# Reordering the front of an attention and top-1 MoE kernel: casts, clears, slot list, unread products and a nested general path

## The chip, the cores and the metric

The kernel runs on one core of a Trainium2 chip. The metric is the device time of one execution in microseconds. It is quoted as the median of several runs. The profile comes from one of these runs. Its times count from the start of its span, which is some 1.7 us shorter than the device time. Every run also lists the clock that TensorE was granted.

## The reference

Attention with two separate softmaxes feeds a top-1 mixture of experts.

```python
# q, k, v: (8 batches, 8 heads, 576, 64), fp32
q_s = softmax(q, over the 64 features);  k_s = softmax(k, over the 576 positions)
kv = einsum('bhsd,bhse->bhde', k_s, v)
x = einsum('bhsd,bhde->bhse', q_s, kv)  -> reshaped to (4608 tokens, 512)

logits = x @ w_gate + modality_bias[modality_id]      # 8 experts, 2 modalities
e_idx = argmax(logits);  gate_w = softmax(logits)[e_idx]
out[token] = gate_w * (relu(x @ w1[e_idx]) @ w2[e_idx])   # 512 -> 1024 -> 512
```

With this draw the modality bias decides the expert, so two experts serve all tokens. The kernel's fast path holds just these two. A general path over all experts stands at the end of the program and is entered only if a check on the chip fails. It runs zero times here.

## The kernel before

For each of the eight batches the program does the following. `prep` computes `exp(k)` and `exp(q)` on ACT and casts v to bf16. `attend` forms the kv product on TensorE (PE), scales it on DVE (`kvbd`), turns q (`tp_ps` to `et`) and kv (`kvT_ps` to `kvT`), and from these the gate products `g_ps` and the logits `lg_ps`. `route` picks the expert, counts the tokens (`r_ps`), scales the tokens (`x_sb`), sorts them by a permutation product (`xT_ps`), and ACT copies them into windows of the sorted buffer `xs`, one expert from the left and one from the right. `slots` and `places` make the list that says where each row of the output goes (`hv`, `hlo`, `id_ps`). The FFN is 148 pieces of PE work on `xs`, called by `mains(n)` or spread by `weave` among the steps of a batch. PE is programmed in a fixed order, so a piece that waits holds all behind it.

The parts that the change touches (`...` marks a cut):

```python
    xs = persist.tile([P, KD, NSLOT], BF16)          # 128 x 4 x 4864: the sorted tokens
    ...
    def clear(b):                                     # zero places of batch b, both sides
        lo, hi = S * b, min(S * (b + 1), NSLOT // 2)
        xs_w[b] = [
            nc.gpsimd.memset(xs[:, :, c : c + hi - lo].bitcast(FP32), 0.0) for c in (lo, NSLOT - hi)
        ]
    clear(0)
    clear(1)
    ...
    def cast_weights(s, part, eng):                   # fp32 stage buffer -> bf16 W, 128 x 2048
        copy_on(eng, W[:, s, part * 2 * F : (part + 1) * 2 * F], wst.pop((s, part))[:, 0 : 2 * F])
    ...
    steps(a1, 4)
    token_ids()
    cast_weights(0, 0, nc.gpsimd)
    for _ in range(NT - 1):
        steps(r0, 1)                                  # batch 0 sorted
        steps(a1, 1)                                  # batch 1 attended
    alone(r0)
    cast_weights(0, 1, nc.scalar)
    alone(a1)
    mains(1)                                          # the first FFN piece
    r1 = route(1)
    cast_weights(0, 2, nc.scalar)
    ...
    steps(r1, 1)
    slots(0)                                          # slot list of batch 0
    cast_weights(1, 0, nc.gpsimd)
    for b in range(2, 5):
        clear(b)                                      # six memsets in a row
    mains(1)
    places(0)                                         # the product that reads slots(0)
    mains(1)
    weave([next(r1)], 0.6)
    cast_weights(1, 1, nc.vector)
    weave(r1, 0.6)
    cast_weights(1, 2, nc.scalar)
    cast_weights(1, 3, nc.scalar)
    mains(12 - now[0])
    slots(1)
    ...
    with tc.For_i(0, nr) as e:                        # general path: nr is 0 here
        ...
        for _, _, lo, w in passes:                    # unrolled: 19 column groups
            hT = hbuf.tile([P, KF, GW], BF16, name="hT")
            alone(ffn1(xs[:, :, lo : lo + w], w, weights_of(0)[0], hT))
            alone(ffn2(w, weights_of(0)[1], hT, lambda: rows_of(sel1, lo, w), "stores again"))
```

The softmax here doesn't subtract the row's maximum and nothing guards it: scores larger than these inputs give would overflow.

## Time and profile before

| | before |
|---|---|
| device time, median of 3 runs | 267.23 us (265.94 to 267.35) |
| span of the profiled run | 265.6 us |
| PE busy | 200.6 us, 76% |
| DVE, ACT, GpSimd busy | 57%, 58%, 30% |
| PE busy between 45 and 60 us | 6.7 of 15 us |

PE is the bound for most of the span, so the time to win is where PE waits or runs at half clock. The row of busy tenths by slice shows that this is the first quarter. The marks to follow are the kv products: each batch begins with 36 of them, so their start times tell how far the program has come.

### The profile page before, as it was taken

The page shows a single profiled execution, that of the slowest core. Times are in us where ns is not written, and L with a number is a line of the kernel's source. Part 1 is how long each engine was busy: PE and PEld are TensorE (multiplying, and loading weights), DVE is VectorE, ACT ScalarE, POOL GpSimd, SP SyncE. Part 2 cuts the span into 40 slices and gives each one's busy share as a digit, 9 for nine tenths or more (in the row PEclk, how much of TensorE's full clock was granted, in tenths as well). Part 3 has the DMA queues.
Part 4 walks back from the last instruction along what each step waited for, and adds up shares of the span by engine and source line. Part 5 has one row for each costly group of instructions (what it writes and reads, how often), then busy time and mean ns, then how long its engine had stood idle before and what let it go on. Part 6 is the DMA issues. An engine that isn't in the chain of part 4 may idle for free. (4 is left out here: it accounts for less than half of the span.)

```text
span 265.6 us, 5231 instructions
## 1 busy us (share of the span) xinstructions
PE 200.6 (76%) x1934; PEld 137.4 (52%) x1954; DVE 151.4 (57%) x501; ACT 153.8 (58%) x241; POOL 78.7 (30%) x94
## 2 busy tenths in 40 slices
PE   0465668447898978898797899888788979999900
PEld 0354545135666447545565575566456637676500
DVE  7488573783043848876793967579385855311110
ACT  2977378138798559666666777665744634443300
POOL 8301000765114216022602341180142052141410
PEclk9995557759799999999999999999999999999975
DMA  6999999566999942861774010210102003030210
GB/s 233 371 390 404 393 391 321 200 206 234 356 389 343 355 174 50 346 237 64 238 246 172 2 79 0 81 79 2 42 12 111 0 39 121 0 158 2 110 57 1
DMA packets 18940, 46.58 MB, mean 175 GB/s; under 512 B 1229, under 2 KB 1229, under 8 KB 18910
## 3 DMA queue, kind: packets, MB, share of 16 engines
q1 hardware_dynamic: 15920, 36.70, 38.9%
q0 software_dynamic: 2960, 9.44, 8.8%
q8 instruction: 17, 0.28, 0.4%
q14 instruction: 13, 0.11, 0.1%
q10 hardware_dynamic: 30, 0.05, 0.1%
HBM read 36.75 MB, written 9.70 MB: 175 GB/s over the span
## 5 line engine op out<-in xcount | busy, mean ns | idle before, releaser
L726 PE MATMUL h_ps<-xs,W 128*128 128x256 bf16 x576 | 74.2, 282 | 4.7 <-ACT hT L737 2.7
L744 PE MATMUL y_ps<-W,hT 128*128 128x512 bf16 x268 | 68.9, 386 | 1.3 <-issue 0.3
L757 POOL DMA_INDIRECT out_dram<-y_sb,ix x37 | 36.7, 991 | 111.9 <-DVE y_sb L358 29.9
L726 PEld LDWEIGHTS <-W 128*128 128x128 bf16 x576 | 55.7, 101 | 14.3 <-issue 3.6
L737 ACT ACTIVATE hT<-h_ps 128x512 bf16<-128x512 f32 x73 | 42.0, 596 | 21.1 <-PE h_ps L726 20.3
L629 ACT CAST xs<-xT_ps 128x512 f32 (+2 forms) x80 | 38.8, 563 | 13.6 <-PE xT_ps L617 13.3
L744 PEld LDWEIGHTS <-hT 128*128 128x128 bf16 x296 | 26.9, 98 | 25.2 <-issue 1.1
L358 ACT COPY y_sb<-y_ps 128x512 f32<-128x512 f32 x22 | 12.9, 586 | 43.2 <-PE y_ps L744 40.9
L580 DVE TENSOR_TENSOR x_sb<-x_ps,qi 128x512 bf16<-128x512 f32 (+1 forms) x40 | 29.8, 764 | 1.2 <-PE x_ps L509 0.5
L358 DVE COPY y_sb<-y_ps 128x512 f32<-128x512 f32 x15 | 10.4, 692 | 33.0 <-PE y_ps L744 33.0
L659 POOL TENSOR_TENSOR hv<-hhi,vals 128x570 bf16<-128x570 bf16 x8 | 12.5, 1568 | 46.3 <-DVE hhi L655 42.5
L617 PE MATMUL xT_ps<-perm,x_sb 128*128 128x128 bf16 (+1 forms) x160 | 16.6, 232 | 9.2 <-DVE x_sb L580 6.6
L617 PEld LDWEIGHTS <-x_sb 128*128 128x128 bf16 (+1 forms) x160 | 10.9, 106 | 19.3 <-DVE x_sb L580 15.2
L376 ACT ACTIVATE ek<-st 128x1152 bf16<-128x1152 f32 x16 | 18.6, 1172 | 1.6 <-DMA st<-in_k_dram 1.6
L376 ACT ACTIVATE eq<-st 128x1152 bf16<-128x1152 f32 x16 | 18.4, 1158 | 0.6 <-DMA st<-in_q_dram 0.6
L509 PE MATMUL x_ps<-kvbd,et 128*128 128x128 bf16 (+1 forms) x160 | 17.5, 239 | 0.4 <-DVE et L358 0.4
L393 PE MATMUL kv_ps<-vb,ek 64*128 64x129 bf16 x288 | 12.8, 239 | 5.9 <-DVE vb L358 2.8
L429 PE MATMUL tp_ps<-ident,eq 128*128 128x128 bf16 x144 | 13.6, 241 | 4.1 <-DVE x_sb L580 2.4
L429 PEld LDWEIGHTS <-eq 128*128 128x128 bf16 x144 | 11.3, 109 | 9.1 <-issue 5.9
L393 PEld LDWEIGHTS <-ek 64*128 64x128 bf16 x288 | 10.3, 104 | 9.7 <-issue 7.6
L358 POOL CAST vb<-st 128x1152 bf16<-128x1152 f32 x12 | 13.5, 1152 | 0.0
L509 PEld LDWEIGHTS <-et 128*128 128x128 bf16 (+1 forms) x160 | 11.8, 109 | 3.3 <-issue 2.2
(148 smaller groups left out, 217.4 us busy)
## 6 DMA issues: line engine op xcount, KB each, us to landing
st<-in_k_dram SPq DMA_DIRECT2D x8, 1152.0 KB, 5.9
st<-in_moe_w_dram SPq DMA_DIRECT2D x8, 1024.0 KB, 12.6
st<-in_v_dram SPq DMA_DIRECT2D x7, 1152.0 KB, 6.3
st<-in_q_dram SPq DMA_DIRECT2D x6, 1152.0 KB, 5.7
st<-in_q_dram SPq DMA_DIRECT2D x4, 576.0 KB, 12.9
st<-in_v_dram SPq DMA_DIRECT2D x2, 576.0 KB, 8.1
out_dram<-y_sb,ix POOLq DMA_INDIRECT x37, 2.8
W<-in_moe_modality_id_dram ACTq DMA_DIRECT2D x1, 36.0 KB
```

Of the source, the lines that this page charges most:

```text
L358: return (nc.scalar.copy if eng is nc.scalar else eng.tensor_copy)(out=out, in_=in_)
L376: nc.scalar.activation(out=view((eks if nm == "k" else eqs)[b], [[Dh, 2], [HG * Dh, NJ], [1, Dh]], 2 * g * Dh), in_=src[:, 2 * g : 2 * g + ...
L393: nc.tensor.matmul(out=kv[hg][:, 130 * hp : 130 * hp + 129], lhsT=ek[rows, j, P * hp : P * hp + P], rhs=vb[rows, j, hp, 0:129], start=(j = ...
L429: nc.tensor.transpose(out=view(tp[c0], [[2 * nj * 64, 2], [1, 64]], hp * nj * 64 + jj * 64), in_=eq[:, c0 + jj, P * hp : P * hp + P], iden ...
L509: nc.tensor.matmul(out=view(x_ps, [[2 * Dh, 2], [1, Dh]], (4 * (p_ % 2) + p_ // 2) * Dh, (0, T)), lhsT=et[:, p_, tcol[t] : tcol[t] + T], r ...
L580: nc.vector.tensor_tensor(out=view(x_out[t], [[2 * Dh, HG], [Dh, 2], [1, Dh]], 0, (0, T)), in0=view(xps[t], [[2 * Dh, HG], [Dh, 2], [1, Dh ...
L617: nc.tensor.matmul(out=xT_ps[:, kd, 0:T], lhsT=x_out[t][0:T, kd * P : (kd + 1) * P], rhs=perm[0:T, t, 0:T], start=True, stop=True,)
L629: w = nc.scalar.copy(out=window(a + off, b, T, off > 0), in_=xT_ps[:, :, 0:T])
L726: nc.tensor.matmul(out=h_ps[:, f * w : (f + 1) * w], lhsT=w1(kd * F + (f0 + f) * P, P), rhs=x_in[:, kd, :], start=(kd == 0), stop=(kd == K ...
L737: nc.scalar.activation(out=h_out, in_=h_in, func=ACT.Relu)
L744: nc.tensor.matmul(out=y_ps, lhsT=hT[:, kf, t * P : (t + 1) * P], rhs=w2(kf * D, D), start=(kf == 0), stop=(kf == KF - 1),)
L757: store = nc.gpsimd.indirect_dma_start(out=out, out_offset=bass.IndirectOffsetOnAxis(ap=ix[:, t : t + 1], axis=0), in_=y_sb, in_offset=Non ...
```

## The change

The intent is to fill the holes of the first 75 us: weight casts go from ACT to idle GpSimd, the clears leave the middle of the program, the slot list of batch 0 is made earlier, and products whose result nobody reads keep PE busy in its waits. The general path is made small by a nested loop. The FFN pieces are also spread a little differently.

```diff
-    clear(0)
-    clear(1)
+    xs_w = [nc.gpsimd.memset(xs[:, kd, :].bitcast(FP32), 0.0) for kd in (2, 3)]
+    xs_w.append(nc.scalar.copy(out=xs[:, 0, :].bitcast(FP32), in_=view(modf, [[0, NSLOT // 2]])))
+    xs_w.append(nc.vector.memset(xs[:, 1, :].bitcast(FP32), 0.0))
 ...
-        tps, tag = (ff, "ff") if b == 0 else (mm, "mm")
+        tps, tag = (ff, "ff") if b < 2 else (mm, "mm")
-        yield 3
+        yield 2.6
-        yield 5
         scale(1)
+        yield 4.2
-            yield 1.2 if t < NT - 1 else 1.3
+            yield 1.4 if t < NT - 1 else 2
 ...
+    def busy(n):
+        junk = ff.tile([P, 512], FP32, name="junk", tag="ff")
+        for _ in range(n):
+            nc.tensor.matmul(out=junk[:, 0:P], lhsT=ones, rhs=tri, start=True, stop=True)
 ...
     r0 = route(0)
+    busy(12)
     steps(r0, 1)
+    busy(10)
 ...
     steps(a1, 4)
+    cast_weights(0, 0, nc.gpsimd)
+    cast_weights(0, 1, nc.gpsimd)
 ...                                   (steps of r0 and a1 with busy(4) to busy(6) between)
     token_ids()
+    slots(0)
     steps(a1, 1)
+    busy(6)
     alone(a1)
+    busy(12)
+    cast_weights(0, 2, nc.scalar)
     mains(1)
     r1 = route(1)
     steps(r1, 1)
-    mains(1)
+    mains(2)
     cast_weights(0, 3, nc.scalar)
     steps(r1, 1)
-    mains(2)
-    steps(r1, 1)
-    slots(0)
-    cast_weights(1, 0, nc.gpsimd)
-    for b in range(2, 5):
-        clear(b)
-    mains(1)
     places(0)
     mains(1)
-    weave([next(r1)], 0.6)
-    cast_weights(1, 1, nc.vector)
-    weave(r1, 0.6)
-    cast_weights(1, 2, nc.scalar)
-    cast_weights(1, 3, nc.scalar)
-    mains(12 - now[0])
+    cast_weights(1, 0, nc.gpsimd)
+    cast_weights(1, 1, nc.gpsimd)
+    steps(r1, 1)
+    mains(2)
+    cast_weights(1, 2, nc.gpsimd)
+    cast_weights(1, 3, nc.gpsimd)
+    weave(r1, 0.8)
     slots(1)
+    mains(14 - now[0])
 ...
-            if i == 6 and b > 2:
+            if i == 7 and b > 2:
                 places(b - 1)
-        weave(batch(b), (14 if b == 2 else 15.5) / 28.6, ...)
+        weave(batch(b), (12 if b == 2 else 15.5) / 28.9, ...)
 ...                                   (general path)
-        for _, _, lo, w in passes:
+        with tc.For_i(0, NSL, GW // P) as at:
+            x_in = hbuf.tile([P, KF, GW], BF16, name="hT")[:, 0:KD, :]
+            nc.vector.tensor_copy(out=x_in, in_=xs[:, :, ds(at * P, GW)])
+            sel2 = small.tile([P, GW // P], FP32, name="sel2")
+            nc.vector.tensor_copy(out=sel2, in_=sel1[:, ds(at, GW // P)])
             hT = hbuf.tile([P, KF, GW], BF16, name="hT")
-            alone(ffn1(xs[:, :, lo : lo + w], w, weights_of(0)[0], hT))
-            alone(ffn2(w, weights_of(0)[1], hT, lambda: rows_of(sel1, lo, w), "stores again"))
+            alone(ffn1(x_in, GW, weights_of(0)[0], hT))
+            alone(ffn2(GW, weights_of(0)[1], hT, lambda: rows_of(sel2, 0, GW), "stores again"))
```

## The prediction

> **What bounds the kernel now.** I first read the busy tenths by slice on the page.
>
> ```profile
> PE   0465668447898978898797899888788979999900
> ...
> PEclk9995557759799999999999999999999999999975
> ```
>
> A slice is 6.64 us. From slice 11 on TensorE (PE) is 80 to 90% busy at full clock; before that it is half idle and mostly at half clock. The table of stretches sizes both regimes.
>
> ```profile
> 45.00:52.00 7.00, 2.85 (x16) 0.99 (x14) 5.03 (x17) 0.58 (x2) 3.90 (x3) 0.89 0.70 271
> 52.00:60.00 8.00, 3.88 (x27) 2.47 (x25) 7.04 (x6) 3.13 (x7) 5.27 (x7) 0.50 0.65 184
> ...
> 125.00:150.00 25.00, 20.65 (x219) 13.93 (x220) 18.21 (x55) 17.02 (x29) 7.34 (x7) 1.00 0.51 174
> ...
> 225.00:250.00 25.00, 24.84 (x184) 16.77 (x186) 5.61 (x13) 10.42 (x18) 5.84 (x6) 1.00 0.15 61
> ```
>
> Columns: length, busy us of PE, PE weight load, DVE, ACT, POOL, then PE clock, DMA share, GB/s. The end (225 to 253) is dense FFN. The middle (six batches, 75 to 222) has PE 83 to 88% busy. In 45 to 60 PE works 6.7 of 15 us. The chain of waits is no help: it stops at the last store. So I went through the timeline of the front.
>
> ```profile
> 22.61 2.22 PE L393 MATMUL kv_ps<-vb,ek 64*128 64x129 bf16 x36 [0.42 <-ACT vb L358]
> ...
> 38.12 1.46 PE L726 MATMUL h_ps<-xs,W 128*128 128x256 bf16 x6 [1.70 <-ACT W L358]
> ...
> 49.80 0.52 PE L676 MATMUL id_ps<-hv,hlo 64*128 64x114 bf16 x5 [4.10 <-POOL hv L659]
> ...
> 51.52 4.56 POOL L228 MEMSET xs<- 128x1152 f32 x6
> ...
> 52.01 4.09 DVE L690 TENSOR_SCALAR ix<-sel 128x2 int32<-128x2 f32 x1
> ...
> 56.19 0.61 PE L617 MATMUL xT_ps<-perm,x_sb 128*128 128x128 bf16 x4 [3.52 <-DVE x_sb L580]
> ...
> 67.29 6.19 PE L726 MATMUL h_ps<-xs,W 128*128 128x256 bf16 x40 [2.69 <-ACT hT L737]
> ...
> 75.61 1.20 PE L393 MATMUL kv_ps<-vb,ek 64*128 64x129 bf16 x36
> ```
>
> Columns: start, duration, engine, what, and in brackets the idle time before it with its releaser. Four holes: the first FFN piece waits for a weight cast that stands late in ACT's queue; the slot list waits for `hv`, whose DVE chain (46.7 to 48.8) came too late; six clears of `xs` on GpSimd hold a 2-element DVE instruction for 4.09 us and all behind it; two weight casts on ACT (63.03 to 66.74) hold the ReLU. The first and last lines are the same 36 products, cold and warm: 2.22 against 1.20 us.
>
> **What the Trainium skill says.** (1) "SBUF — State Buffer", section "Who interferes with whom": DVE shares one port pair with GpSimd under an exclusive lock; a 2-port DVE copy or tensor_scalar fully blocks behind any GpSimd operation, one with two SBUF inputs only behind a GpSimd operation that reads. The trace agrees: under the memsets the two-input `ab` took its normal 0.19 us, the tensor_scalar `ix` 4.09; under the W cast at 49.69 the two-input `idb` took 0.90 instead of 0.20. (2) "TensorE: Matmul & The Clock Gate", Part 1: the clock is half until about one 3.4 us window is busy, and falls back after an idle one. The trace agrees: recorded clock 0.50 from 20 to 43 us and again in 52 to 60. (3) "VectorE: DVE Perf Modes", section "Zero memsets can be issued as uint32": a memset takes a cycle per element. Here 256 words took 0.27 us. (4) "Runtime: NRT & Kernel Launch", section "Instruction fetch mechanics": a taken branch beyond the prefetched pages stalls for a fetch. Here GpSimd's branch over the general path, at 257.8, is followed by nothing until 260.5, while the other engines went on.
>
> **The change part by part.**
>
> *Clearing.* All of `xs` is now cleared at the start, one quarter each on DVE and ACT and two on GpSimd. DVE: 2432 words at 0.27/256 = 2.55 us, from 8.0 (after `krow`) to 10.6, so the first `vb` cast moves from 9.10 to 10.6. ACT: copies take 0.59 for 512 and 1.90 for 2048 columns, so about 2.25 us for 2432; it starts at 4.8 where ACT waited 1.6 us for k, so it delays `ek` by 0.7 us. GpSimd: 2 x 2432 against 4 x 1152 words, 4.4 us for 4.14. Net cost on the path: kv products about 1.2 us late, and so everything to the first `lg_ps` (18.9 instead of 17.7), the bias product being moved into a wait. Cost: **+1.2**. What it removes: the memsets at 51.5, i.e. the 3.5 us hole.
>
> *Weight casts.* Seven of eight casts stood on ACT (five), DVE (one, blocked 4.48) and GpSimd (two); now six are on GpSimd at 1.89 each and two on ACT. W part 1 is cast as it lands, near 28 to 30 (estimate: part 0 was there at 25.3, and 1.05 MB at the 398 GB/s of that stretch take 2.6 us), so the 1.70 us wait goes. The last two slot-1 casts leave ACT: the 2.69 us hole goes. Stage buffers come free sooner (the last W load was issued at 38.1 behind ACT's cast), so loads go on.
>
> *Order.* `token_ids` and `slots(0)` move ahead of batch 1's logits: about 0.8 + 2.2 us of DVE, of which about 1.6 delay `gx` and 0.4 us the logits, beyond before; in return `hv` is ready long before its product, the 4.10 us hole goes. The second `x_sb` scaling comes before batch 1's kvbd: its product moves from 29.1 to about 26.8.
>
> *Unread products.* 62 of 128x128, about 0.08 us warm to 0.13 cold: 5 to 8 us of PE, nearly all in waits (22 of them, 2.8 us cold, fill the 3.0 us before r_ps). The last 12 stand straight before the first FFN piece: about +1. In return the clock should hold at 1.0 from some 24 us on: the 16 us of PE work from 20 to 44 shrinks by about 7, of which I count 2 on the path, since ACT (ten window copies of 0.55, `et` 1.0, kvT 0.6) sets the pace there.
>
> By hand, with these durations: r_ps near 23.3; first token product 26; last window copy 34.4 (before 36.3); batch 1 logits 35.7 to 36.2 (35.1 to 35.8); first FFN piece done 38.1 (39.6); DVE held once by the W casts of 36.0 to 39.8 (about 1.7 us at the bias add), batch 1 r_ps 42.0 (44.65); second FFN product done 45.4 (51.8); last window of batch 1 at 53.3 (63.1); twenty pieces done and batch 2's kv at **61.5**. Before, it stood at 75.6 after eighteen; two pieces at 0.87 us make that 77.3. Gain at equal work **15.8 us**. Batch 2 then takes 12 pieces for 14, so the total at its end is equal; I let 0.8 of the gain get lost there: **-15**.
>
> *Middle.* The weights of the weave change. PE's waits from 75 to 225:
>
> ```profile
> PE r_ps L568 <- DVE isa L556: 2.9, 6, 1.1
> PE id_ps L676 <- POOL hv L659: 2.9, 3, 1.6
> PE kv_ps L393 <- ACT xs L629: 2.4, 5, 0.9
> PE xT_ps L617 <- ACT xs L629: 2.3, 2, 1.2
> ```
>
> Columns: total us, times, longest. The new program has four FFN pieces instead of three between lg_ps and r_ps, one between the last two token products, and the slot list a step later; `gx` goes ahead of the list update on DVE. These waits sum to 10.5; a quarter to a half should go, the rest reappears elsewhere: **-3**. Pieces left after the last batch are the same 38, so the dense end keeps its length.
>
> *General path.* It does not run; its body falls from 128 to about 60 GpSimd instructions and from 1891 to about 120 on PE. GpSimd's 2.7 us fetch gap at the end may go: I count **-1**.
>
> Sum: 267.2 - 15 - 3 - 1 = 248.2; hand chains miss waits, so I add 1.8: **250.0 us**.
>
> **Rivals.** (a) *GpSimd becomes the bound of the front.* Six casts (11.3 us) plus stores in order: the casts of the last two parts stand behind the first store, near 47 to 51, and are needed near 57 on my chain; DVE operations with two SBUF inputs wait behind each. Against it: in 47 to 51 DVE reads PSUM. If casts come late, the gain halves: about 258. (b) *The front is bound by loads or by ACT.* DMA share is 1.04 until 36 us at about 400 GB/s; loads up to batch 2's q are 19 MB (6 + 3 inputs of 1.18, 8 parts of 1.05), 49 us at that rate, before the 53 to 61 where they are needed. So it is hidden but not by much; if not, 254 to 256. (c) *Lost time is given back in the middle.* If batches 2 to 7 were paced by a transfer or by DVE's 74%, arriving 15 us sooner would only move the wait; DMA there falls from 0.83 to 0.11, so I don't believe it: about 262 if so. (d) *The unread products delay the real ones*, by a slot of PSUM: xT now shares three buffers with them and with batch 1's turns, so it is in fact single-buffered. I have that in the chain; if worse, +2.
>
> **Range and chances.** The four removed holes (12.0 us at their ends) are well seen; the middle is a guess of 0 to -6, the tail 0 to -2.7, the start +0.5 to +2. That gives 245 to 257. Under 261.9 (2%) unless (c) or (a) at its worst: 0.95 faster, 0.04 same, 0.01 slower.
>
> **What would show it.** Right: clock near 1.0 from about 25 us; first `vb` cast near 10.6; no DVE instruction of 4 us; id_ps for batch 0 without a wait; batch 2's kv near 61; kv of consecutive batches 23.5 us apart (24.0 before). Wrong: W casts on GpSimd waiting for DMA or behind a store past 57 us; kv of batch 2 after 68; batches now further apart; clock still 0.5 after 30, which would say the small products don't count as activity.

## The result and the profile after

The changed kernel takes **250.49 us** (median of 4 runs, 250.11 to 251.3), against 267.08 us (median of 4, 265.94 to 267.35) for the kernel before on the same chip. The ratio is 0.9391, with a 95% interval of 0.9354 to 0.9427. A ratio is the mean time of one kernel's fast runs over that of the other's of the same rounds, so it is not quite the ratio of the medians. Where microseconds are given for a difference of ratios below, the difference is multiplied by 267.1.

The page's busy tenths of the changed kernel, 40 slices of 6.22 us each:

```profile
PE   0078569899878889797989888986998789999960
PEclk9999997999979999999999999999999999999995
```

PE is now busy for seven tenths or more of nearly every slice from 6 on (37 us), where this began at slice 9 (60 us) before. The clock row has lost the fives of the front, but it can't be taken at its word there: time ahead of a trace's first clock record is counted as full, and in this trace that record, a step to full clock, comes at 24.1 us. The products show the pace before it: 18 kv products take 1.16 us at 13.18 us and 0.68 at 62.50. After it, only slices 6 and 11 dip. The first slices are emptier than before: two zeros stand where there were a zero and a four.

The table of stretches of the changed kernel, in the columns explained in the prediction:

```profile
45.00:52.00 7.00, 6.21 (x53) 3.48 (x51) 5.31 (x14) 4.51 (x9) 2.92 (x2) 1.00 1.06 391
52.00:60.00 8.00, 7.95 (x70) 6.24 (x67) 5.87 (x14) 5.53 (x10) 5.62 (x5) 1.00 1.04 397
...
125.00:150.00 25.00, 21.40 (x233) 14.81 (x233) 18.14 (x57) 16.69 (x29) 7.76 (x7) 1.00 0.24 88
```

From 45 to 60 us PE is busy for 14.2 us instead of 6.7. The middle is nearly as it was, 21.40 against 20.65 of 25 us.

The timeline of the changed kernel at the four places where PE waited before, and at batch 2's kv:

```profile
38.89 1.91 PE L719 MATMUL h_ps<-xs,W 128*128 128x256 bf16 x8
...
43.36 0.53 PE L669 MATMUL id_ps<-hv,hlo 64*128 64x114 bf16 x5
...
47.52 0.29 PE L610 MATMUL xT_ps<-perm,x_sb 64*128 64x64 bf16 x4 [0.73 <-DVE x_sb L573]
...
53.25 5.40 PE L719 MATMUL h_ps<-xs,W 128*128 128x256 bf16 x48
...
62.50 0.68 PE L386 MATMUL kv_ps<-vb,ek 64*128 64x129 bf16 x18
```

No idle time stands ahead of the first FFN piece (1.70 us before), of the slot list (4.10) or of the later pieces (2.69). The clears are gone from the middle, and of the 3.52 us that PE waited there for `x_sb`, 0.73 is left. The kv product of batch 2 starts at 62.50, with 20 pieces done.

The start tells another story. First the timeline of the kernel before, from 4.69 to 10.01 us:

```profile
4.69 1.26 DVE L273 CAST parts<-left 1x16 bf16<-1x16 f32 x1
...
6.08 0.90 DVE L275 CAST parts<-key 1x2 bf16<-1x2 f32 x1
...
10.01 1.16 PE L393 MATMUL kv_ps<-vb,ek 64*128 64x129 bf16 x18 [2.82 <-DVE vb L358]
```

Then the same part of the changed kernel:

```profile
4.69 2.33 DVE L266 CAST parts<-left 1x16 bf16<-1x16 f32 x1
4.88 4.21 POOL L223 MEMSET xs<- 128x2432 f32 x2
...
7.15 1.96 DVE L268 CAST parts<-key 1x2 bf16<-1x2 f32 x1
...
10.33 2.08 DVE L850 MEMSET xs<- 128x2432 f32 x1 [0.45 <-issue]
...
13.18 1.16 PE L386 MATMUL kv_ps<-vb,ek 64*128 64x129 bf16 x18 [3.86 <-DVE vb L351]
```

Two casts of 16 and 2 elements take 2.33 and 1.96 us. Each lasts until one of GpSimd's two memsets ends (the first near 7.0, the second at 9.09), where the shorter memsets of the kernel before held them for 1.26 and 0.90. So DVE comes to its own memset at 10.33. The first value cast starts at 12.33 instead of 9.10, and the first kv product at 13.18 instead of 10.01.

The time by stretches, from the start times of the kv products (us):

| stretch | before | after | change | predicted |
|---|---|---|---|---|
| start to kv of batch 3 (31 pieces done before, 32 after) | 96.10 | 85.34 | -10.8 | -15 |
| kv of batch 3 to kv of batch 7 | 94.87 | 94.46 | -0.4 | |
| kv of batch 7 to the end of the last product | 61.51 | 60.57 | -0.9 | -3 with the row above |
| last product to the end of the span | 13.1 | 8.6 | -4.5 | -1 |
| allowance for missed waits | | | | +1.8 |
| sum | 265.6 | 249.0 | -16.6 | -17.2 |

The first two columns are span times and the predicted column is device time, so only differences are compared. The pieces are counted from the products in the traces. The changed kernel stays one piece ahead at every mark from batch 3 on, so at equal work, with 0.87 us a piece as in the prediction, the first row is -11.6 and the third about 0. The sum agrees and the terms do not. Two more places explain terms: batch 2 and the end.

Batch 2 in the timeline of the changed kernel:

```profile
64.00 0.69 PE L386 MATMUL kv_ps<-vb,ek 64*128 64x129 bf16 x18 [0.81 <-POOL vb L351]
...
68.14 1.17 ACT L369 ACTIVATE ek<-st 128x1152 bf16<-128x1152 f32 x1
69.69 0.60 ACT L440 COPY kvT<-kvT_ps 128x512 bf16<-128x512 bf16 x1
70.34 0.25 PE L463 MATMUL g_ps<-wg_sb,kvT 128*128 128x8 bf16 x4 [1.70 <-ACT kvT L440]
...
71.83 1.80 PE L737 MATMUL y_ps<-W,hT 128*128 128x512 bf16 x4
```

The second half of the kv product waits for a value cast that stands behind a store in GpSimd's queue. The gate product waits 1.70 us for the `kvT` copy, which stands behind an exp of 1.17 us and a ReLU in ACT's queue. Then four products of 128x512 take 1.80 us, where four take 1.03 us some four microseconds later: the clock record is at half from 71.9 to 75.3. That half-clock window is not the main loss: in a_lateclear the clock is full from 36.3 to 241 us, and its batch 2 takes 22.57 us against 22.84 here.

The end of the program, from the view of the general path's loop line (engine, operation, count, then shortest, median and longest duration in ns, first and last start). Before:

```profile
L1011 POOLq EVENT_SEMAPHORE  x16: 17/43/43, 256.5 to 261.5; - x16
...
L1011 PEldq COMPARE_BRANCH  x3: 101/196/4027, 249.1 to 259.1; - x3
```

After:

```profile
L1023 POOLq EVENT_SEMAPHORE  x15: 17/43/124, 242.1 to 244.8; - x15
...
L1023 PEldq COMPARE_BRANCH  x3: 96/174/188, 237.0 to 245.2; - x3
```

One branch on PE's sequencer took 4.03 us before and none takes over 0.19 us after. GpSimd's last semaphore comes 9.0 us after the last product before (261.5 less 252.5) and 4.4 us after it now (244.8 less 240.4). Before, GpSimd's branches at 254.0 and 257.8 were followed by nothing until 256.5 and 260.5 (2.4 and 2.7 us); now no such gap stands between its branches at 242.0 and 244.9. PE's long branch, from 252.7 to 256.7, lay beside the first of these gaps.

### The profile page after: what moved, and what is told of

The parts are those of the page before. It is cut to its first block, busy times and chain, and to the rows that moved or that the text cites. A ratio compares the mean times of both kernels' runs of the same rounds, so it can differ in the third digit from the quotient of the medians.

```text
span 249.0 us, 5372 instructions
## 1 busy us (share of the span) xinstructions
PE 197.4 (79%) x2016; PEld 137.5 (55%) x2016; DVE 155.9 (63%) x507; ACT 148.0 (59%) x233; POOL 81.8 (33%) x90
## 5 line engine op out<-in xcount | busy, mean ns | idle before, releaser
L750 POOL DMA_INDIRECT out_dram<-y_sb,ix x37 | 36.6, 989 | 115.0 <-DVE y_sb L351 36.3
L737 PE MATMUL y_ps<-W,hT 128*128 128x512 bf16 x288 | 71.7, 385 | 0.1
L719 PE MATMUL h_ps<-xs,W 128*128 128x256 bf16 x576 | 70.6, 274 | 0.1
L719 PEld LDWEIGHTS <-W 128*128 128x128 bf16 x576 | 54.5, 98 | 7.1 <-issue 0.4
L730 ACT ACTIVATE hT<-h_ps 128x512 bf16<-128x512 f32 x69 | 40.6, 597 | 28.0 <-PE h_ps L719 26.2
L351 DVE COPY y_sb<-y_ps 128x512 f32<-128x512 f32 x17 | 11.8, 692 | 35.1 <-PE y_ps L737 32.4
L351 ACT COPY y_sb<-y_ps 128x512 f32<-128x512 f32 x20 | 11.7, 585 | 31.7 <-PE y_ps L737 30.1
L573 DVE TENSOR_TENSOR x_sb<-x_ps,qi 128x512 bf16<-128x512 f32 (+1 forms) x40 | 26.2, 681 | 1.9 <-PE x_ps L502 1.2
L610 PE MATMUL xT_ps<-perm,x_sb 128*128 128x128 bf16 (+1 forms) x160 | 14.8, 214 | 13.1 <-DVE x_sb L573 10.1
L351 POOL CAST W<-st 128x2048 bf16<-128x2048 f32 x6 | 11.4, 1924 | 17.3 <-DMA st<-in_moe_w_dram 17.3
L502 PE MATMUL x_ps<-kvbd,et 128*128 128x128 bf16 (+1 forms) x160 | 16.3, 229 | 0.0
## 6 DMA issues: line engine op xcount, KB each, us to landing
st<-in_q_dram SPq DMA_DIRECT2D x4, 576.0 KB, 13.1
```

What stands on the lines that cost most here:

```text
L351: return (nc.scalar.copy if eng is nc.scalar else eng.tensor_copy)(out=out, in_=in_)
L502: nc.tensor.matmul(out=view(x_ps, [[2 * Dh, 2], [1, Dh]], (4 * (p_ % 2) + p_ // 2) * Dh, (0, T)), lhsT=et[:, p_, tcol[t] : tcol[t] + T], r ...
L573: nc.vector.tensor_tensor(out=view(x_out[t], [[2 * Dh, HG], [Dh, 2], [1, Dh]], 0, (0, T)), in0=view(xps[t], [[2 * Dh, HG], [Dh, 2], [1, Dh ...
L610: nc.tensor.matmul(out=xT_ps[:, kd, 0:T], lhsT=x_out[t][0:T, kd * P : (kd + 1) * P], rhs=perm[0:T, t, 0:T], start=True, stop=True,)
L719: nc.tensor.matmul(out=h_ps[:, f * w : (f + 1) * w], lhsT=w1(kd * F + (f0 + f) * P, P), rhs=x_in[:, kd, :], start=(kd == 0), stop=(kd == K ...
L730: nc.scalar.activation(out=h_out, in_=h_in, func=ACT.Relu)
```

## The experiments

All twelve runs gave correct results. Each stands beside runs of the kernel before on its own chip. Labels with `a_` and `best_` start from the changed kernel, those with `b_` from the kernel before.

### a_unrolled: the general path unrolled again

```diff
-        with tc.For_i(0, NSL, GW // P) as at:
-            x_in = ...; sel2 = ...
+        for _, _, lo, w in passes:
```

> The changed kernel with the general path unrolled again (it does not run in either form). My theory: the end of the program paid for the size of that body, TensorE's branch over it took 4.03 us and GpSimd's was followed by 2.7 us of nothing, and the time from the last product to the end of the span went from 13.2 to 8.6 us. So this kernel is 4 to 5 us slower than the changed one, about 254.9, with nothing different before the last product. The rival: the shorter end has to do with the state of the stores, not the body; then it stays at 250.5 and the end at 8.6 us.

Measured: 255.94 us (254.67 to 258.56), ratio 0.9555 (0.9507 to 0.9603). One of the four runs, the profiled one at 258.56, fell in the slow state; the median counts it, the ratio does not, and its trace is not used. Undoing this part costs 0.0164 of 267.1, or 4.4 us.

### b_nested: the nested path alone, in the kernel before

```diff
-        for _, _, lo, w in passes:
+        with tc.For_i(0, NSL, GW // P) as at:
+            x_in = ...; sel2 = ...
```

> The kernel before with only the general path nested. If the body's size is the cause, 4 to 5 us faster than the kernel before, about 262.5, the last product still near 252.5 us and the end after it near 8.6 us instead of 13.2. The rival (the end depends on the rest): 267.

Measured: 263.78 us (262.42 to 264.36), ratio 0.9847 (0.9797 to 0.9898), a gain of 4.1 us. Its last product ends at 253.56, 1.1 us later than in the kernel before, and the span ends 9.2 us after that instead of 13.1. Both ways of isolating this part give the same answer. The long branch on PE goes with the body too: it takes 3.95 us in b_newclear, which keeps the unrolled body, and no branch on PE takes over 0.33 us in any of the eleven traces with the nested one. The code that never runs cost some 4 us at the end.

### a_quiet: no unread products

```diff
     def busy(n):
-        junk = ff.tile([P, 512], FP32, name="junk", tag="ff")
-        for _ in range(n):
-            nc.tensor.matmul(out=junk[:, 0:P], lhsT=ones, rhs=tri, start=True, stop=True)
+        return
```

> The changed kernel without the 62 unread products. Prediction's theory: they hold the clock at 1.0 from 24 us on, worth about 2 us on the path net of their own time, so 251.5 to 253.5, with a recorded clock of 0.5 between 24 and 37 us. Rival: they stand on the path more than they help (the last 12 stand straight before the first FFN piece, 1.4 us), then 248 to 250. Second rival: the front is paced by ACT, DVE and loads, so that neither clock nor products matter: within 0.7 us of 250.5.

Measured: 251.96 us (250.4 to 252.55), ratio 0.9407 (0.9354 to 0.946) against 0.9391. The difference of 0.4 us is well inside the intervals. PE is busy for only 1.79 of the 4 us from 20 to 24 (3.67 with the products). The clock column says 1.00 from 20 to 37 us in both, but the first clock record comes at 24.1 us in the changed kernel and at 34.5 here, and time ahead of it is counted as full. The kv products of batch 1 show the real pace, first in the changed kernel, then in this run, then in a_oldweave, which keeps the products:

```profile
25.28 0.69 PE L386 MATMUL kv_ps<-vb,ek 64*128 64x129 bf16 x18 [0.50 <-ACT vb L351]
...
25.26 2.21 PE L386 MATMUL kv_ps<-vb,ek 64*128 64x129 bf16 x36 [0.42 <-ACT vb L351]
...
25.28 2.22 PE L386 MATMUL kv_ps<-vb,ek 64*128 64x129 bf16 x36 [0.49 <-ACT vb L351]
```

In the kernel before, 36 of them took 2.22 us at a recorded clock of 0.50 and 1.20 at 1.00. So without the products this front ran at half clock until 34.5 us. With them the profiled run of the changed kernel was at full clock from 24.1, but a_oldweave only from 35.6 and a_casts from 33.5. The products do not bring the clock up reliably, and whether they did in the changed kernel is not shown. Nor does the time follow: the first FFN piece starts at 38.26 us without them and at 38.89 with them.

### a_oldweave: the old spreading of the pieces

```diff
-        yield 2.6
+        yield 3
-        yield 4.2
+        yield 5
-            yield 1.4 if t < NT - 1 else 2
+            yield 1.2 if t < NT - 1 else 1.3
-            if i == 7 and b > 2:
+            if i == 6 and b > 2:
-        weave(batch(b), (12 if b == 2 else 15.5) / 28.9, ...)
+        weave(batch(b), (12 if b == 2 else 15.5) / 28.6, ...)
```

> The changed kernel with the old weights of the weave (3, 5, 1.2, 1.3, the list a step earlier). My prediction gave the new weights 3 us; the traces show 1.35 us from batch 3's kv to the last product and a new wait of g_ps for ACT's kvT copy (4.3 us in all). If the new weights are worth what the traces show, 251.5 to 252.5; if they were worth 3, 253.5; if the new wait eats all, 250.5 or less.

Measured: 251.3 us (250.03 to 251.94), ratio 0.9382 (0.9335 to 0.9429). No difference shows, though this run's front was at half clock for 11 us longer (see a_quiet). From the kv of batch 3 to that of batch 7 it takes 180.19 less 85.53, or 94.66 us, against 94.46 with the new weights. The new spreading brought nothing that these runs can see.

### a_casts: three weight casts back on ACT

```diff
-    cast_weights(0, 1, nc.gpsimd)
 ...
+    cast_weights(0, 1, nc.scalar)
     cast_weights(0, 2, nc.scalar)
 ...
-    cast_weights(1, 2, nc.gpsimd)
-    cast_weights(1, 3, nc.gpsimd)
     weave(r1, 0.8)
+    cast_weights(1, 2, nc.scalar)
+    cast_weights(1, 3, nc.scalar)
```

> The changed kernel with three of the six GpSimd weight casts put back on ACT in their old places (slot 0 part 1 ahead of part 2; slot 1 parts 2 and 3 behind batch 1's routing). Theory: ACT's queue holds the first FFN piece by one cast (1.9 us) and then the ReLUs by two (3.8 us, a wait of some 2.7 us), so batch 2's kv comes 3 to 5 us later and the time is 253 to 255. Rival: loads set when batch 2 can start, DMA share being 1.04 up to 60 us; then the later release of two load buffers adds more, 256 or over; or the waits are hidden and it stays under 251.5.

Measured: 252.87 us (252.38 to 253.08), ratio 0.9458 (0.9426 to 0.9491), a loss of 1.8 us; the intervals just touch. The kv of batch 2 comes at 63.69 instead of 62.50. The casts on GpSimd help, but by less than the holes of 1.70 and 2.69 us that they stood for.

### a_oldclear: the old clears in the changed kernel

```diff
-    xs_w = [nc.gpsimd.memset(xs[:, kd, :].bitcast(FP32), 0.0) for kd in (2, 3)]
-    xs_w.append(nc.scalar.copy(...)); xs_w.append(nc.vector.memset(...))
+    clear(0)
+    clear(1)
 ...
     cast_weights(1, 0, nc.gpsimd)
+    for b in range(2, 5):
+        clear(b)
```

(Each batch's first copy into `xs` waits for that batch's clears again.)

> The changed kernel with the old clears on GpSimd: two batches at the start, the other three behind the first slot-1 weight cast. Two effects against each other. At the start the first kv product comes near 10.0 to 10.5 instead of 13.18, because DVE's two small casts wait 2.1 us less for the shorter memsets and DVE has no memset of its own: -3 us there. Later the six memsets (4.6 us) hold DVE's two-port instructions and the second slot-1 cast: +3 to +5. I expect 250 to 253 in all, with batch 0's r_ps near 21.5. The prediction's step (clears cost 1.2 at the start and save 3.5 later) would say about 253.

Measured: 247.28 us (247.22 to 248.19), ratio 0.9265 (0.923 to 0.9299): **3.4 us faster** than the changed kernel. The first kv product starts at 9.84 instead of 13.18, which is 3.3 us earlier. The six memsets in the middle are back, yet they hold nothing for long. The timeline of this run:

```profile
40.72 4.64 POOL L229 MEMSET xs<- 128x1152 f32 x6 [2.39 <-PE r_ps L571]
40.81 0.98 DVE L574 TENSOR_SCALAR gsum<-gsum 128x5 f32<-128x5 f32 x1
```

A DVE operation of the same kind as the `ix` that took 4.09 us before is now held for 0.98, about one memset, and later ones for 0.39 and less. So this part of the change cost time, though the prediction counts its hole among those that are well seen.

### a_lateclear: all four quarters on GpSimd, after DVE's value casts

```diff
-    xs_w = [nc.gpsimd.memset(...) for kd in (2, 3)]
-    xs_w.append(nc.scalar.copy(...)); xs_w.append(nc.vector.memset(...))
+    xs_w = []
 ...
     steps(p0, 4)
+    for kd in range(KD):
+        xs_w.append(nc.gpsimd.memset(xs[:, kd, :].bitcast(FP32), 0.0))
+    after(xs_w[0], v_casts[-1:], "the clears come behind the value casts")
```

> The changed kernel with all four quarters of the clear on GpSimd, held until DVE's second value cast of batch 0, in the time from 12 to 21 us in which GpSimd has nothing to do; none on DVE or ACT. Theory (the memsets at 4.9 us cost the start 3 us, through the port lock on DVE's small casts and DVE's own memset): those casts take 0.15 us each, the first kv product stands near 10.0, batch 0's logits near 17.3 instead of 20.3, and the time is 2 to 4 us less, about 247.5. Rival: loads (share 1.04 up to 60 us) set batch 2's start, then the 3 us turn into waits for weights and the time stays within 0.7 us of 250.5.

Measured: 247.5 us (247.09 to 248.19), ratio 0.9271 (0.9235 to 0.9306), 3.2 us faster than the changed kernel. The timeline of this run:

```profile
4.69 0.27 DVE L265 CAST parts<-left 1x16 bf16<-1x16 f32 x1
...
5.09 0.15 DVE L267 CAST parts<-key 1x2 bf16<-1x2 f32 x1
...
9.96 1.16 PE L387 MATMUL kv_ps<-vb,ek 64*128 64x129 bf16 x18 [4.51 <-DVE vb L352]
...
11.29 8.33 POOL L865 MEMSET xs<- 128x2432 f32 x4 [6.35 <-DVE vb L352]
```

The same two casts take 0.27 and 0.15 us when no memset runs beside them. This confirms the reading of the start: the first kv product comes 3.22 us earlier and the whole program ends 3.2 us earlier.

### a_lateslots: the slot list of batch 0 behind batch 1's routing again

```diff
     token_ids()
-    slots(0)
 ...
     steps(r1, 1)
-    places(0)
     mains(1)
+    steps(r1, 1)
+    slots(0)
     cast_weights(1, 0, nc.gpsimd)
     cast_weights(1, 1, nc.gpsimd)
-    steps(r1, 1)
-    mains(2)
+    mains(1)
+    places(0)
+    mains(1)
```

> The changed kernel with the slot list of batch 0 (eight DVE instructions and hv on GpSimd) put back behind batch 1's routing, its product still ahead of the sixth FFN piece as in the kernel before. My prediction: that list came too late for its product and cost TensorE a wait of 4.10 us; so this kernel is 3 to 5 us slower than the changed one, near 254.5, with id_ps waiting 2 to 4 us for hv. Rival: in the new order something else is late there too (x_sb behind perm, the ReLU behind a cast), and the list hides in it: under 252.

Measured: 256.57 us (255.37 to 257.73), ratio 0.9613 (0.9549 to 0.9677), a loss of 5.9 us. (The edit also moves one step of batch 1's routing and two casts, so the 5.9 us are those of the group.) The hole comes back in its timeline:

```profile
48.86 0.74 PE L669 MATMUL id_ps<-hv,hlo 64*128 64x114 bf16 x5 [4.70 <-POOL hv L652]
```

The products now take 0.74 instead of 0.53 us, and the clock row of this run's page has a six in the slice from 44.6 to 51.0 us. So the wait costs more than its own length. The kv of batch 2 starts at 67.05, 4.6 us late. Of the parts tried alone this is worth most.

### b_newclear: the new clearing alone, in the kernel before

```diff
-    clear(0)
-    clear(1)
+    xs_w = [nc.gpsimd.memset(xs[:, kd, :].bitcast(FP32), 0.0) for kd in (2, 3)]
+    xs_w.append(nc.scalar.copy(...)); xs_w.append(nc.vector.memset(...))
 ...
-    for b in range(2, 5):
-        clear(b)
```

> The kernel before with the change's clearing alone. The prediction had +1.2 at the start and -3.5 for the hole under the memsets, so 265. With what the runs show of the start (+3.0 to the first kv product) and if the hole under the memsets at 51.5 goes whole: 266.5 to 267.5, the first kv product near 13.2 and no DVE instruction of 4 us in batch 1's routing. Rival, from the changed kernel with the old clears being 3.3 us faster: the later memsets never cost their 3.5 us on the path, then 269.5 to 270.5.

Measured: 266.19 us (265.62 to 268.16), ratio 0.9996 (0.9928 to 1.0064). The start loses 3.2 us (first kv product at 13.18 instead of 10.01), and the kv of batch 2 comes 1.0 us earlier (74.57), so the middle gained 4.2 us. That is about the removed hole. The total does not resolve the 1.0 us that is left. In the old order the gain was there, and the cost at the start ate most of it; in the new order there was no gain left to set against the cost.

### best_no12: late clears, without the twelve products ahead of the first FFN piece

```diff
     alone(a1)
-    busy(12)
     cast_weights(0, 2, nc.scalar)
```

> Late clears, without the 12 unread products that stand straight before the first FFN piece (1.44 us in the trace of the late clears, from 33.5 to 34.8, with nothing else for TensorE to wait for). If that stretch is on the path, 246.0 to 246.6; if the next wait (isa behind a weight cast on GpSimd, r_ps at 41.1 there) sets the pace, no change: 247.2 to 247.8.

Measured: 249.21 us (247.15 to 249.63), ratio 0.9313 (0.925 to 0.9376), against 0.9271 for a_lateclear. No gain; the intervals overlap. The first FFN piece starts at 33.99 instead of 34.76, and the next wait takes it back:

```profile
41.41 0.17 PE L562 MATMUL r_ps<-isa,tri 128*128 128x5 bf16 x1 [2.63 <-DVE lst L673]
```

The counts of batch 1 come at 41.41, against 41.09 in a_lateclear. DVE sets the pace here, not PE: its `isa`, which this product reads, took 1.91 us (38.85 to 40.76) beside a weight cast on GpSimd, where it takes 0.23 elsewhere. The profiled run's batch 2 takes 24.22 us against 22.57 in a_lateclear, with the clock at half from 76.3 to 79.7, so its time is no clean measure of the twelve products.

### best_kvt: as best_no12, with the kvT copies of batches 2 to 7 on DVE

```diff
-            nc.scalar.copy(out=kvT, in_=kvT_ps[:, 0 : NP * P])
+            copy_on(nc.vector if b > 1 else nc.scalar, kvT, kvT_ps[:, 0 : NP * P])
```

> The same with the kvT copy of batches 2 to 7 on DVE, where ACT stood with an exp ahead of it (g_ps waited 4.3 us for it in five batches of the changed kernel, DVE idle 2.75 us in the first of them). If these waits are on the path of the batches, 3 to 4 us less, about 243.5; if the chain then waits for something else (x_sb, or ACT's window copies ahead of the next kv), 0 to 1.5 less.

Measured: 246.48 us (246.33 to 246.68), ratio 0.9239 (0.919 to 0.9287), 2.0 us better than best_no12 on the same chip. Batch 2 takes 22.2 us from its kv product to the next (59.15 to 81.36), where it took 24.2 in best_no12 (60.00 to 84.22). The profiled runs differ by 3.3 us; 0.85 of it stands before that batch, where the two kernels are the same. Half-clock windows fall at different places in the two (73.2 to 76.6 and 76.3 to 79.7), so best_both tests this again.

### best_both: late clears, the twelve products kept, kvT on DVE

```diff
     (a_lateclear, and)
-            nc.scalar.copy(out=kvT, in_=kvT_ps[:, 0 : NP * P])
+            copy_on(nc.vector if b > 1 else nc.scalar, kvT, kvT_ps[:, 0 : NP * P])
```

> The changed kernel with all four clears on GpSimd behind DVE's second v cast, its twelve unread products ahead of the first FFN piece kept, and the kvT copies of batches 2 to 7 on DVE. Theory (the two gains add: late clears -3.2 us, and kvT on DVE -2.0 us, as it was worth beside the run without the twelve products): 245.0 to 246.0, ratio 0.917 to 0.921 to the kernel before, and no g_ps wait on ACT kvT over 0.6 us. Rival (the -2.0 was noise of the run without the twelve products, whose own times spread over 2.5 us; DVE is as late with kvT as ACT was): 247.0 to 247.6, ratio 0.926 to 0.928.

Measured: 243.48 us (242.6 to 244.17, 6 runs), ratio 0.9214 (0.9191 to 0.9237). The chip of this run is faster for the kernel before too (264.61 us, where the other chips gave 267.0 to 267.5), so the ratio is what counts. It is 0.0057, or 1.5 us, below a_lateclear's, and 0.0177, or 4.7 us, below the changed kernel's; the intervals of best_both and a_lateclear just touch. In batch 2 neither of these two has a half-clock window: it takes 20.71 us here (59.72 to 80.43) and 22.57 in a_lateclear, which is 1.9 us for `kvT` on DVE. These two ran on different chips; best_kvt and best_no12, on one chip, gave 2.0. The ratio lies at the upper edge of the expected 0.917 to 0.921, and the rival's 0.926 is outside the interval. The intervals of best_kvt and best_both overlap, so which of the two is better stays open. Both beat the changed kernel and the kernel before. PE's waits from 60 to 210 us in this run (total us, times, longest):

```profile
PE xT_ps L611 <- DVE x_sb L574: 8.4, 10, 2.0
...
PE g_ps L464 <- DVE kvT L352: 0.9, 1, 0.9
```

The same view of a_lateclear has 4.3 us of `g_ps` waiting for ACT's `kvT`. Of these 3.4 us, 1.5 reach the end. The largest wait left, PE for DVE's `x_sb`, is 8.4 us in both.

## Why the prediction was right, and where it was not

The predicted time (250.0) and the measured one (250.49) differ by 0.5 us. The range held. The mechanism of the main gain, holes of the front filled by work placed earlier, was right. The total was also lucky: four terms were mis-sized, and their errors cancel. Against the predicted -17.2, at equal work, the front with batch 2 fell short by 3.4 and the middle by 2.5; the end gave 3.5 more, and the allowance of 1.8 was not needed. This makes -16.6.

**The holes, right.** All four went but for 0.73 us, and batch 2's kv came at 62.50 where 61.5 was predicted. At equal work that is 14.8 us (77.3 less 62.5) for a predicted 15.8. The slot list was worth 5.9 us and three of the casts 1.8 by experiment. The price was foreseen as well: the bias add of batch 1, predicted to be held for about 1.7 us by the weight casts, took 1.71 (39.85 to 41.56).

**The start, mis-sized.** The step "DVE: ... from 8.0 (after `krow`) to 10.6, so the first `vb` cast moves from 9.10 to 10.6" failed. It moved to 12.33. DVE reached its memset at 10.33, 2.3 us late, since two tiny casts were held by GpSimd's longer memsets: 2.33 + 1.96 less (1.26 + 0.90) is 2.1 us. I had read this rule from the trace for the middle and did not apply it to the clears that the change puts at the start. The memset itself took 2.08 us, not 2.55. (The sum as written, 2432 times 0.27/256, gives 2.57, and "Seven of eight casts" should read eight; nothing rests on either.) The cost was 3.2 us instead of 1.2 at the kv product and 2.6 at the first `lg_ps` (20.33 against 17.70). a_lateclear and a_oldclear give 3.2 and 3.4 us back when this is undone.

**"What it removes: ... the 3.5 us hole", wrong in this order.** It holds for the kernel before (b_newclear: 4.2 us gained after the start). In the changed kernel the same six memsets cost DVE 0.98 us once (a_oldclear), so clearing early saved little and cost 3.4 net. I had credited a part with a hole that another part of the change would have closed.

**Batch 2, mis-sized.** "I let 0.8 of the gain get lost there" measured 3.2: at equal work the gain fell from 14.8 at its kv to 11.6 at the next. With 12 pieces it took 22.84 us, against 20.49 with 13 before (the count of 14 in my text was one too high). The trace shows the waits for `vb` (0.81) and `kvT` (1.70) and a half-clock window after them. The `kvT` part is shown by experiment: with the copy on DVE, the batch takes 2.0 us less in best_kvt than in best_no12, and 1.9 less in best_both than in a_lateclear. The window cost 0.3 here, from a_lateclear's 22.57; it may cost more where it falls later, as in best_no12. The wait for `vb` is read from the trace and was not tried alone.

**The middle, mis-sized.** "-3" measured -1.4, and 0.9 of that is the one piece more that was done before, so about -0.5 at equal work. The step that failed was that a quarter to a half of the listed waits would go by the new weights. a_oldweave shows that the weights do nothing measurable. The waits did not shrink but changed names. PE's waits from 60 to 210 us in the changed kernel:

```profile
PE xT_ps L610 <- DVE x_sb L573: 6.6, 9, 1.1
PE g_ps L463 <- ACT kvT L440: 4.3, 5, 1.7
PE xT_ps L610 <- ACT xs L622: 2.8, 3, 0.9
```

The slot list no longer waits for GpSimd's `hv`, and the wait for `x_sb`, 2.2 us from 75 to 222 before, is now 6.6. The spacing of the batches was predicted as 23.5 us and came out as 23.6. The same reckoning over batches 3 to 7 gives 23.7 before (94.87 by 4), not the 24.0 of my text, so hardly anything changed here.

**The end, mis-sized.** "GpSimd's 2.7 us fetch gap at the end may go: I count -1" measured -4.5. I had counted one gap of GpSimd, and only a part of it. There was a second one of 2.4 us (254.0 to 256.5), and both went. PE's own branch, which took 4.03 us, I had not looked at. By the prediction's count the unrolled body had 1891 PE instructions and has some 120 now. a_unrolled and b_nested put the part at 4.4 and 4.1 us. PE's stall ended at 256.7, beside GpSimd's first gap, so which of the two held that stretch was not separated; in the second gap GpSimd stood alone.

**The unread products.** I counted 2 us for the clock and a cost of 1. In the total nothing measurable is left of either: 0.4 us, inside the noise. The predicted sign "clock near 1.0 from about 25 us" came true in the profiled run (24.1 us), but not in a_oldweave (35.6) and a_casts (33.5), which have the same products there; without them it was 34.5. The step "the clock should hold at 1.0 from some 24 us on" was thus right once and not as a rule. In those two runs the prediction's own sign of being wrong appeared, a clock still at half after 30 us, and the time did not show it.

**The rivals.** GpSimd as the bound (a) shows only as the 0.81 us at `vb`; loads (b) do not appear among PE's waits there, though GpSimd's first two casts waited for theirs (1.03 us ahead of the second); the middle gave nothing back (c), since batches 3 to 7 kept their spacing.

**What stays open.** Single undoings give: nested path 4.4, slot list 5.9, casts 1.8, clears -3.4, products 0.4, weights -0.2, together 8.9 of the 16.3 us that 1 less 0.9391 makes of 267.1. The remaining 7.4 belong to the rest of the order (scaling of tokens before `kvbd`, the PSUM pool of batch 1's turns, the order of the pieces, the first cast) or to parts acting together, as the clears show they do. Open too is what sets the moment at which the clock rises in the front. Also open is why one DVE operation waited through all six memsets in the kernel before and through one in a_oldclear.

## What to carry to other kernels

Look first for work that a queue does too late: making one small list earlier was worth more than moving three casts or adding unread products. Before moving bulk clears, list what the engine that shares a port with the clearing one does at that moment, down to the 2-element casts. Code that is never entered can cost time where the program branches over it, and a total that agrees does not show that its terms do: check each at marks in the trace, at equal work. Check a clock column against the durations of equal products, above all ahead of the first clock record.

## What the Trainium skill lacked or had wrong

- "SBUF — State Buffer", section "Who interferes with whom", says that the loser of the shared port waits until the other has finished. It does not say whether a waiting DVE operation gets in between GpSimd operations that follow each other. Here it went both ways: 4.09 us through six memsets in the kernel before, 0.98 us beside six memsets in a_oldclear, and 2.33 us (one of two memsets) at the changed kernel's start.
- "Runtime: NRT & Kernel Launch", section "Instruction fetch mechanics", gives no size for the stall of a taken branch that leaves the fetched window. If the branches over the general path are such (the trace does not name the cause), one took 4.03 us on PE, two on GpSimd were followed by 2.4 and 2.7 us of nothing, and the smaller loop body made the program 4.1 to 4.4 us shorter.
- "VectorE: DVE Perf Modes", section "Zero memsets can be issued as uint32", says a cycle for each element. The time does grow with the elements, but the section names no fixed part. Here 4 elements took 0.06, 256 words 0.27 and 2432 words 2.08 us, which fits 0.06 us plus 0.83 ns per element. Scaling the 0.27 up, as I did, gave 2.55.
